# Finer first weight loads and a new order of the first and last steps in a fused attention and ELU kernel

## The chip, the cores and the metric

The kernel runs on one core of one Trainium2 chip. The metric is the device time of one execution in microseconds (us), lower is better. The profile's own span is about 1.7 us shorter than that time. PE is TensorE, PEld its weight loads, ACT is ScalarE, DVE VectorE, POOL GpSimd (which here issues loads and makes masks) and SP SyncE (which issues stores and the loads of q and k). All times inside a trace count from the start of its span.

The runs named r1 were made on one chip, r2 on a second and r3 on a third; medians are compared within one chip.

## The reference

Attention with a window of 32 on either side, then a two-layer network with ELU between its layers:

```python
scores = q @ k.T / sqrt(64); scores = where(|i - j| <= 32, scores, -1e9)
x = softmax(scores) @ v                       # 8 batches x 8 heads x 576 rows x 64
h = x.reshape(4608, 512) @ w_in               # 512 -> 2048
out = where(h > 0, h, exp(min(h, 0)) - 1) @ w_out     # 2048 -> 512
```

## The kernel before

The network part is a chain of 144 steps. A step is a tile of 256 tokens and two of the sixteen blocks of 128 hidden units. It has a first-layer product (`mm1`, 8 matmuls), an exponential (ACT), "minus one" (DVE), an ELU (DVE) and a second-layer product (`mm2`, 4 matmuls). Attention for later tokens is woven in between. PSUM has two tiles for first-layer results, taken in turn, so the `mm1` of step n must wait for the ELU of step n-2.

```python
    def mm1(kk):                      # cut
        ...                           # 8 matmuls: ps <- w_in_sb, xT
        nc.scalar.activation(e_sb, ps, AX.Exp)
        if kk == 1: nc.scalar.activation(m_sb, e_sb, AX.Copy, bias=-1.0)
        else:       nc.vector.tensor_scalar(m_sb, e_sb, -1.0, None, ALU.add)
    ...
    for kk in range(NSTEP + LAG):
        run(kk, "first")
        if 1 <= kk < NSTEP: elu(kk - 1)
        run(kk, "dve")                # attention work for DVE
        if kk < NSTEP: mm1(kk)
        run(kk, "mid")                # scores, values' products, fillers ...
        for n in {2: (), 3: (0, 1), 4: (), 5: (2, 3)}.get(kk, ...): mm2(n)
        run(kk, "end")
```

Steps 0 to 3 use the first 256 tokens, which are pairs 0 and 1 of the attention. Steps 4 to 7 use pairs 2 and 3, whose attention must be finished in between. The weights come by casting loads (float32 to bf16), a quarter of each matrix per load, all issued from POOL into one queue. "Fillers" (`idle`) are matmuls on zeros, meant to keep PE's clock up.

The softmax here doesn't subtract the row's maximum and nothing guards it: scores larger than these inputs give would overflow.

Of the kernel before, what the change touches and what calls it, by code (L numbers as in the profile page):

```python
# [21 lines left out]
def kernel(  # L22
# [9 lines left out]
    nc = tc.nc  # L32
# [6 lines left out]
    D_FF = moe_w_in.shape[1]  # L39
# [7 lines left out]
    VS = 5  # L47
# [5 lines left out]
    NFO = D_FF // 128  # L53
    FG = 2
    STEPS = NFO // FG
# [38 lines left out]
    def ps_tile(shape, dt, tag, name):  # L94
        return pools[tag].tile(shape, dt, tag=tag, name=name)
# [11 lines left out]
    w_out_sb = wpool.tile([128, NFO, D_MODEL], BF16, name="w_out_sb")  # L107
# [20 lines left out]
    def load_cast(b, which, part):  # L128
        z, nj = part
        t = cpool.tile([128, 2, nj * D], BF16, tag=f"c{which}",  # L130
                       name=f"c{which}")
        qk_c[b, which, z] = t
        src = (q, k)[which][b, :, z * NC * nj:(z + 1) * NC * nj, :].rearrange(
            "(g h) (c j) d -> c g h (j d)", h=2, j=nj)
        for h in range(2):
            nc.gpsimd.dma_start(out=t[:, h, :], in_=src[:, :, h, :])  # L136

    def load_v(b, m):
        lo = 128 * m - WIN
        p0 = max(0, -lo)  # L140
        p1 = min(128, S - lo)
        nc.gpsimd.dma_start(  # L142
            out=V_e[b % 3][p0:p1, m, :, 0:D],
            in_=v[b, :, lo + p0:lo + p1, :].rearrange("h p d -> p h d"))
# [25 lines left out]
        t = cpool.tile([1, 1], dt, name=f"gate{gates[0]}")  # L170
        eng.dma_start(out=t, in_=src)

    def load_w_in(c):
        w = D_FF // 4
        nc.gpsimd.dma_start(
            out=w_in_sb[:, :, c * w:(c + 1) * w],
            in_=moe_w_in[:, c * w:(c + 1) * w].rearrange(
                "(o p) f -> p o f", p=128))

    def load_w_out(c):  # L180
        n = NFO // 4
        nc.gpsimd.dma_start(
            out=w_out_sb[:, c * n:(c + 1) * n, :],
            in_=moe_w_out[c * n * 128:(c + 1) * n * 128, :].rearrange(
                "(o p) f -> p o f", p=128))
# [46 lines left out]
    def copy_on(eng, d_, s_):  # L232
        if eng is nc.scalar:
            nc.scalar.copy(d_, s_)  # L234
        else:
            eng.tensor_copy(d_, s_)  # L236
# [165 lines left out]

    for which in range(2):
        load_cast(0, which, HALF_B)
    load_w_in(0)
    for mi in (0, 4):
        nc.gpsimd.affine_select(
            out=masks[:, mi, :], in_=masks[:, mi, :], compare_op=ALU.is_ge,
# [4 lines left out]
        channel_multiplier=-1)  # L413
    for m in (3, 4):
        load_v(0, m)
    load_w_in(1)
    load_w_out(0)
    load_w_out(1)

    idle(10, "y1")  # L420
    front_cast(0, HALF_A, nc.vector)
# [26 lines left out]
    for which in range(2):  # L448
        load_cast(1, which, HALF_A)
    load_w_in(2)  # L450
    load_w_out(2)
    for m in range(3):
        load_v(1, m)
# [15 lines left out]
    def at(kk, slot, fn, *args):  # L469
        tasks.setdefault((kk, slot), []).append((fn, args))  # L470

    def run(kk, slot):
        for fn, args in tasks.get((kk, slot), ()):
            fn(*args)
# [9 lines left out]

    at(0, "mid", scores, 2, "s")
    at(0, "mid", scores, 3, "u")
    for i in (2, 3):
        at(0, "mid", exponential, i)
    for i in (2, 3):
        at(0, "mid", rotate_v, 0, 2, VS - 1, (i - 2,))  # L490
        at(0, "mid", mask, i)

        at(1, "mid", idle, (4, 2)[i - 2], "y1")
        at(1, "mid", pv, i)
        at(2, "dve", normalize, i)
        at(3, "mid", x_transpose, i)
        at(3, "mid", x_evac, i, nc.scalar)
    at(1, "end", idle, 1, "y1")
    at(4, "dve", swap_pools)

    for part, kq in ((HALF_A, 7), (HALF_B, 15)):
# [20 lines left out]
    for i in range(4, NPAIR):  # L522
        two = i >= FIRST_TWO
        kk, z = begin[i], i % 2 if two else 0
# [5 lines left out]
        n = kk + (3 + z if two else 2)  # L530
# [55 lines left out]
    psH, m_t, g_t, psY = {}, {}, {}, {}  # L586

    def mm1(kk):
        t, s = order[kk]
        h = kk % 2  # L590


        tags = (f"h{h}", "s") if kk == NSTEP - 1 else (f"h{h}",)
        w = FG // len(tags)
        psH[kk], m_t[kk] = [], []
        for z, tag in enumerate(tags):
            ps = ps_tile([128, w, TT], FP32, tag, "ps")
            psH[kk].append(ps)
            for j in range(w):
                fo = s * FG + z * w + j  # L600
                for do in range(NDO):
                    nc.tensor.matmul(  # L602
                        ps[:, j, :],
                        lhsT=w_in_sb[:, do, fo * 128:(fo + 1) * 128],
                        rhs=xT[t][:, :, do, :],
                        start=(do == 0), stop=(do == NDO - 1))
        for z, ps in enumerate(psH[kk]):
            e_sb = mpool.tile([128, w, TT], FP32, tag="e_sb", name="e_sb")
            nc.scalar.activation(e_sb, ps, AX.Exp)  # L609
            m_sb = mpool.tile([128, w, TT], BF16, tag="m_sb", name="m_sb")  # L610
            if kk == 1:

                nc.scalar.activation(m_sb, e_sb, AX.Copy, bias=-1.0)
            else:
                nc.vector.tensor_scalar(m_sb, e_sb, -1.0, None, ALU.add)  # L615
            m_t[kk].append(m_sb)
            if kk == NSTEP - 1:
                elu(kk, z)

    def elu(kk, z=0):  # L620
        if z == 0:
            g_t[kk] = mpool.tile([128, FG, TT], BF16, tag="g_sb", name="g_sb",
                                   bufs=5)
        ps = psH[kk][z]
        w = ps.shape[1]
        nc.vector.scalar_tensor_tensor(  # L626
            g_t[kk][:, z * w:(z + 1) * w, :], ps, 0.0, m_t[kk][z],
            ALU.max, ALU.min)

    out_t = out.rearrange("(t ts p) c -> t p ts c", p=128, ts=TT // 128)  # L630

    def mm2(kk, parts=(0, 1)):
        t, s = order[kk]
        if s == 0:
            psY[t] = [ps_tile([128, D_MODEL], FP32, g, "psY")
                      for g in (("h2", "t0") if t == 1 else ("y0", "y1"))]
        last = t == NT - 1 and s == STEPS - 1
        for ts in parts:
            for j in range(FG):
                nc.tensor.matmul(  # L640
                    psY[t][ts],
                    lhsT=g_t[kk][:, j, ts * 128:(ts + 1) * 128],
                    rhs=w_out_sb[:, s * FG + j, :],
                    start=(s == 0 and j == 0),
                    stop=(s == STEPS - 1 and j == FG - 1))
        if last and s == STEPS - 1:


            for ts in parts:
                for z in range(1 + ts):  # L650
                    c = slice(z * D_MODEL // 2 * ts,
                              D_MODEL if z == ts else D_MODEL // 2)
                    eng = (nc.vector, nc.scalar)[z]
                    y_sb = opool.tile([128, D_MODEL], FP32,
                                      tag=f"y_sb{1 - z}", name="y_sb")
                    copy_on(eng, y_sb[:, c], psY[t][ts][:, c])
                    (nc.scalar if z else nc.sync).dma_start(
                        out_t[t, :, ts, c], y_sb[:, c])
        elif s == STEPS - 1:
            for ts in range(2):  # L660
                eng = (nc.scalar, nc.vector)[ts]
                y_sb = opool.tile([128, D_MODEL], FP32, tag=f"y_sb{ts}",
                                  name="y_sb")
                copy_on(eng, y_sb, psY[t][ts])
                nc.sync.dma_start(out_t[t, :, ts, :], y_sb)

    LAG = 2
    for kk in range(NSTEP + LAG):
        run(kk, "first")
        if 1 <= kk < NSTEP:  # L670
            elu(kk - 1)
        run(kk, "dve")
        if kk < NSTEP:
            mm1(kk)
        run(kk, "mid")

        for n in {2: (), 3: (0, 1), 4: (), 5: (2, 3)}.get(
                kk, (kk - LAG,) if kk >= LAG else ()):

            if n < NSTEP - 2:  # L680
                mm2(n)
            elif n == NSTEP - 1:
                for ts in range(2):
                    for m in (n - 1, n):
                        mm2(m, (ts,))
        run(kk, "end")


# [28 lines left out]
```

## Time and profile before

| | before |
|---|---|
| median of the first three timed runs | 305.61 us |
| the execution that was profiled | 306.17 us, span 304.5 |
| PE busy | 296.0 us, 97% |
| DVE, ACT busy | 80%, 55% |

Read it so: PE has work nearly all the time, so what counts is when its unbroken stretch begins and what follows its end.

### The profile page before, as it was taken

The page shows a single profiled execution, that of the slowest core. Times are in us where ns is not written, and L with a number is a line of the kernel's source. Part 1 is how long each engine was busy: PE and PEld are TensorE (multiplying, and loading weights), DVE is VectorE, ACT ScalarE, POOL GpSimd, SP SyncE. Part 2 cuts the span into 40 slices and gives each one's busy share as a digit, 9 for nine tenths or more (in the row PEclk, how much of TensorE's full clock was granted, in tenths as well). Part 3 has the DMA queues.
Part 4 walks back from the last instruction along what each step waited for, and adds up shares of the span by engine and source line. Part 5 has one row for each costly group of instructions (what it writes and reads, how often), then busy time and mean ns, then how long its engine had stood idle before and what let it go on. Part 6 is the DMA issues. An engine that isn't in the chain of part 4 may idle for free.

```text
span 304.5 us, 7644 instructions
## 1 busy us (share of the span) xinstructions
PE 296.0 (97%) x3091; PEld 197.4 (65%) x3091; DVE 242.2 (80%) x473; ACT 168.6 (55%) x254; POOL 48.6 (16%) x68
## 2 busy tenths in 40 slices
PE   8789999999999999999999999999999999999995
PEld 3456666677676666666666666666667666666662
DVE  6867688978888887988798879887988787877664
ACT  3654556778664567546754675467535353534331
POOL 8836100910003100230013001400000000000000
PEclk9999999999999999999999999999999999999999
DMA  9999999998755997999799969996921111111011
GB/s 191 177 201 205 183 272 413 295 168 182 177 176 158 297 126 187 246 319 157 164 251 303 196 157 268 325 159 116 281 57 71 34 71 34 72 37 69 2 69 70
DMA packets 92117, 52.81 MB, mean 173 GB/s; under 512 B 76594, under 2 KB 81970, under 8 KB 92082
## 3 DMA queue, kind: packets, MB, share of 16 engines
q1 hardware_dynamic: 47330, 35.61, 43.3%
q0 software_dynamic: 42880, 10.10, 40.9%
q10 hardware_dynamic: 1872, 6.62, 5.8%
q8 instruction: 24, 0.39, 0.6%
q14 instruction: 11, 0.09, 0.1%
HBM read 36.70 MB, written 15.34 MB: 171 GB/s over the span
## 4 chain that ended last, share of the span: by engine, by line
PE 90%; DMA 3%; DVE 2%; POOL 2%; ACT 1%; issue 1%; DVEq 0%; POOLq 0%; ACTq 0%
PE ps L602 41%; PE psY L640 40%; PE psS L336 4%; PE psS L304 3%; DMA w_in_sb<-in_moe_w_in_dram 3%; PE ptx L279 1%; POOL Ve L142 1%; POOL c L136 1%; PE psXT L357 1%; DVE g_sb L626 1%; ACT pu L315 1%; DVE pm L324 0%; DVE m_sb L615 0%; PE ptx L274 0%; ACT e_sb L609 0%
## 5 line engine op out<-in xcount | busy, mean ns | idle before, releaser
L609 ACT ACTIVATE e_sb<-ps 128x512 f32<-128x512 f32 (+1 forms) x145 | 86.3, 595 | 120.6 <-PE ps L602 113.0
L602 PE MATMUL ps<-xT,w_in_sb 128*128 128x256 bf16 x1152 | 149.2, 273 | 1.4 <-DMA w_in_sb<-in_moe_w_in_dram 1.4
L640 PE MATMUL psY<-w_out_sb,g_sb 128*128 128x512 bf16 x576 | 147.6, 380 | 0.2 <-DVE g_sb L626 0.2
L602 PEld LDWEIGHTS <-w_in_sb 128*128 128x128 bf16 x1152 | 110.6, 98 | 39.7 <-DMA w_in_sb<-in_moe_w_in_dram 1.9
L626 DVE SCALAR_TENSOR_TENSOR g_sb<-ps,m_sb 128x512 bf16<-128x512 f32 (+1 forms) x145 | 99.4, 686 | 12.6
L615 DVE TENSOR_SCALAR m_sb<-e_sb 128x512 bf16<-128x512 f32 x144 | 62.5, 434 | 38.3 <-ACT e_sb L609 36.5
L640 PEld LDWEIGHTS <-g_sb 128*128 128x128 bf16 x576 | 54.5, 98 | 39.0 <-DVE g_sb L626 0.6
L142 POOL DMA_DIRECT2D Ve<-in_v_dram x40 | 35.4, 897 | 139.7 <-PE psS L336 79.9
L315 ACT ACTIVATE pu<-psS 128x1024 bf16<-128x1024 f32 x36 | 36.5, 1021 | 1.4 <-PE psS L304 1.4
L348 DVE TENSOR_TENSOR x_st<-psS,rc 128x512 bf16<-128x512 f32 x36 | 24.9, 692 | 1.2
L324 DVE TENSOR_TENSOR pm<-pu,masks 128x1024 bf16<-128x1024 bf16 x36 | 24.6, 683 | 0.6 <-ACT pu L315 0.5
L234 ACT CAST qkb<-f 128x768 bf16<-128x768 f32 (+1 forms) x29 | 25.0, 860 | 0.0
L336 PEld LDWEIGHTS <-pm 128*64 128x64 bf16 x576 | 11.2, 111 | 9.9 <-DVE pm L324 8.7
L336 PE MATMUL psS<-Ve,pm 128*64 128x65 bf16 x320 | 13.6, 197 | 0.9 <-DVE pm L324 0.9
L236 DVE COPY y_sb<-psY 128x512 f32<-128x512 f32 (+1 forms) x19 | 12.7, 671 | 1.0 <-PE psY L640 1.0
L304 PEld LDWEIGHTS <-kT 64*128 64x128 bf16 x576 | 9.5, 95 | 4.9 <-issue 4.0
L336 PE MATMUL psS<-Vo,pm 128*64 128x65 bf16 x256 | 12.0, 196 | 0.2 <-DVE Vo L153 0.2
L304 PE MATMUL psS<-qT,kT 64*128 64x64 bf16 x576 | 11.8, 191 | 0.5 <-DVE kT L236 0.5
L234 ACT COPY y_sb<-psY 128x512 f32<-128x512 f32 (+1 forms) x18 | 10.3, 571 | 3.0 <-DVE y_sb L236 3.0
L153 DVE COPY Vo<-Ve 64x1040 bf16<-64x1040 bf16 x24 | 10.3, 431 | 1.5 <-DMA Ve<-in_v_dram 0.8
L395 PE MATMUL ps_idle<-zeros 128*128 128x512 bf16 x27 | 9.5, 482 | 1.3 <-DVE zeros L194 1.3
L234 ACT COPY qT<-ptx 128x1152 bf16<-128x1152 bf16 (+2 forms) x8 | 7.5, 971 | 3.9 <-PE ptx L279 3.0
(36 smaller groups left out, 72.4 us busy)
## 6 DMA issues: line engine op xcount, KB each, us to landing
out_dram<-y_sb SPq DMA_DIRECT2D x35, 256.0 KB, 3.5
f<-in_q_dram SPq DMA_DIRECT2D x12, 576.0 KB, 5.6
f<-in_k_dram SPq DMA_DIRECT2D x12, 576.0 KB, 7.9
in_dram<-qkb ACTq DMA_DIRECT2D x10, 576.0 KB, 3.9
Ve<-in_v_dram POOLq DMA_DIRECT2D x24, 128.0 KB, 11.0
w_in_sb<-in_moe_w_in_dram POOLq DMA_DIRECT2D x4, 512.0 KB, 9.9
w_out_sb<-in_moe_w_out_dram POOLq DMA_DIRECT2D x4, 512.0 KB, 12.8
Ve<-in_v_dram POOLq DMA_DIRECT2D x16, 96.0 KB, 10.5
```

Source lines behind the costliest of these rows:

```text
L142: nc.gpsimd.dma_start(out=V_e[b % 3][p0:p1, m, :, 0:D], in_=v[b, :, lo + p0:lo + p1, :].rearrange("h p d -> p h d"))
L234: nc.scalar.copy(d_, s_)
L304: nc.tensor.matmul(psS[:, h % 2, hp * 128 + z * QB:hp * 128 + (z + 1) * QB], lhsT=kT[b % 2][base:base + 64, KPAD + hp * S + QB * qb - WIN: ...
L315: nc.scalar.activation(pu, _bap(psS, [psS.ap[0], [1, 1024]]), AX.Exp, scale=SCALE)
L324: nc.vector.tensor_mul(pm, pu, _bap(mm, [mm.ap[0], [0, H], [1, 2 * QB]]))
L336: nc.tensor.matmul(psS[QB * z:QB * (z + 1), par, hp * VD:(hp + 1) * VD], lhsT=pm[:, par * HP + hp, z * QB:(z + 1) * QB], rhs=vv[:, qb // 2 ...
L348: nc.vector.tensor_mul(x_st, _bap(psS, [psS.ap[0], [VD, HP], [512, 2], [1, D]]), _bap(rc, [rc.ap[0], [2, HP], [1, 2], [0, D]]))
L602: nc.tensor.matmul(ps[:, j, :], lhsT=w_in_sb[:, do, fo * 128:(fo + 1) * 128], rhs=xT[t][:, :, do, :], start=(do == 0), stop=(do == NDO - 1))
L609: nc.scalar.activation(e_sb, ps, AX.Exp)
L615: nc.vector.tensor_scalar(m_sb, e_sb, -1.0, None, ALU.add)
L626: nc.vector.scalar_tensor_tensor(g_t[kk][:, z * w:(z + 1) * w, :], ps, 0.0, m_t[kk][z], ALU.max, ALU.min)
L640: nc.tensor.matmul(psY[t][ts], lhsT=g_t[kk][:, j, ts * 128:(ts + 1) * 128], rhs=w_out_sb[:, s * FG + j, :], start=(s == 0 and j == 0), sto ...
```

## The change

Intent: the first product waits for a quarter of w_in although it uses an eighth of the matrix. So the first half of each matrix is loaded by eighths, which are just what a step needs. Steps 2 and 3 then go ahead of the values' products of pairs 2 and 3. ELUs 0 and 1 go ahead of pair 3's mask on DVE. Step 2's "minus one" goes to ACT. The second product of step 2 is done before step 4. At the end, one more matmul of the last step but one moves in front of the matmul that waits for the last ELU.

```diff
-    load_w_in(0)
+    for c in (0, 1):
+        load_w_in(c, 8)
 ... # mask selections, values 3 and 4
-    load_w_in(1)
-    load_w_out(0)
-    load_w_out(1)
+    for c in (2, 3):
+        load_w_in(c, 8)
+    for c in range(4):
+        load_w_out(c, 8)
 ...
+    at(0, "mid", exponential, 2)
+    at(1, "dve", rotate_v, 0, 2, VS - 1, (0,))
+    at(1, "dve", mask, 2)
+    at(1, "dve", rotate_v, 0, 2, VS - 1, (1,))
+    at(1, "mid", exponential, 3)
+    at(1, "mid", idle, 5, "y1")
+    at(2, "dve", mask, 3)
+    at(2, "mid", pv, 2)
+    at(2, "mid", normalize, 2)
+    at(3, "mid", pv, 3)
+    at(3, "mid", normalize, 3)
     for i in (2, 3):
+        at(3, "mid", lambda n: mm2(n), i - 2)
         at(3, "mid", x_transpose, i)
         at(3, "mid", x_evac, i, nc.scalar)
 ...
-            if kk == 1:
+            if kk in (1, 2):
 ...
-        for n in {2: (), 3: (0, 1), 4: (), 5: (2, 3)}.get(
+        for n in {2: (), 3: (2,), 4: (), 5: (3,)}.get(
 ...
-                for ts in range(2):
-                    for m in (n - 1, n):
-                        mm2(m, (ts,))
+                mm2(n - 1, ((0, 0), (0, 1), (1, 0)))
+                mm2(n, ((0, 0), (0, 1)))
+                mm2(n - 1, ((1, 1),))
+                mm2(n, ((1, 0), (1, 1)))
```

The old lines that put pairs 2 and 3 into the schedule are cut.

More of the change, by code (lines that the diff above doesn't have):

```diff
@@ L171, in gate, with load_w_in @@
         eng.dma_start(out=t, in_=src)
-    def load_w_in(c):
-        w = D_FF // 4
+    def load_w_in(c, of=4):
+        w = D_FF // of
         nc.gpsimd.dma_start(
@@ L178, in load_w_in, with load_w_out @@
                 "(o p) f -> p o f", p=128))
-    def load_w_out(c):
-        n = NFO // 4
+    def load_w_out(c, of=4):
+        n = NFO // of
         nc.gpsimd.dma_start(
@@ L486 @@
     at(0, "mid", scores, 3, "u")
-    for i in (2, 3):
-        at(0, "mid", exponential, i)
-    for i in (2, 3):
-        at(0, "mid", rotate_v, 0, 2, VS - 1, (i - 2,))
-        at(0, "mid", mask, i)
-        at(1, "mid", idle, (4, 2)[i - 2], "y1")
-        at(1, "mid", pv, i)
-        at(2, "dve", normalize, i)
+    at(0, "mid", exponential, 2)
[9 more added lines that the diff above has]
+    at(3, "mid", normalize, 3)
+    for i in (2, 3):
+        at(3, "mid", lambda n: mm2(n), i - 2)
         at(3, "mid", x_transpose, i)
         at(3, "mid", x_evac, i, nc.scalar)
-    at(1, "end", idle, 1, "y1")
     at(4, "dve", swap_pools)
@@ L630, with mm2 @@
     out_t = out.rearrange("(t ts p) c -> t p ts c", p=128, ts=TT // 128)
-    def mm2(kk, parts=(0, 1)):
+    def mm2(kk, parts=((0, 0), (0, 1), (1, 0), (1, 1))):
         t, s = order[kk]
@@ L637, in mm2 @@
         last = t == NT - 1 and s == STEPS - 1
-        for ts in parts:
-            for j in range(FG):
-                nc.tensor.matmul(
-                    psY[t][ts],
-                    lhsT=g_t[kk][:, j, ts * 128:(ts + 1) * 128],
-                    rhs=w_out_sb[:, s * FG + j, :],
-                    start=(s == 0 and j == 0),
-                    stop=(s == STEPS - 1 and j == FG - 1))
+        for ts, j in parts:
+            nc.tensor.matmul(
+                psY[t][ts],
+                lhsT=g_t[kk][:, j, ts * 128:(ts + 1) * 128],
+                rhs=w_out_sb[:, s * FG + j, :],
+                start=(s == 0 and j == 0),
+                stop=(s == STEPS - 1 and j == FG - 1))
         if last and s == STEPS - 1:
-            for ts in parts:
+            for ts in sorted({ts for ts, _ in parts}):
                 for z in range(1 + ts):
```

## The prediction

> **What bounds the kernel now.** I read the table of stretches first, cutting the span where the timeline shows TensorE change its work. Columns: us, then busy us and count for PE, PEld, DVE, ACT and POOL, then clock, DMA share and GB/s.
>
> ```profile
> 14.80:16.17 1.37, 0.00 (x0) 0.00 (x1) 0.29 (x1) 0.00 (x0) 0.00 (x0) 1.00 2.04 182
> 16.17:21.50 5.33, 5.11 (x88) 3.29 (x89) 3.49 (x7) 3.55 (x5) 2.61 (x4) 1.00 1.28 201
> 21.50:25.57 4.07, 4.07 (x34) 2.79 (x32) 3.79 (x9) 2.16 (x4) 0.86 (x1) 1.00 1.23 207
> 33.25:100.00 66.75, 66.53 (x760) 45.50 (x759) 53.84 (x105) 44.70 (x64) 13.11 (x15) 1.00 1.23 228
> 100.00:200.00 100.00, 100.00 (x1072) 67.47 (x1070) 85.49 (x169) 60.00 (x92) 13.64 (x16) 1.00 1.13 228
> 297.00:304.50 7.50, 3.72 (x21) 1.69 (x19) 3.37 (x8) 1.14 (x3) 0.00 (x0) 0.97 0.20 71
> ```
>
> From 21.5 to 297 us PE is busy practically all the time at full clock, so that stretch is a conveyor: it starts earlier or not. Only the start and the tail can change. At 14.80 us PE stops for 1.37 us. The waits of PE and the chain (start, us, what) name the reason:
>
> ```profile
> PE ps L602 <- DMA w_in_sb<-in_moe_w_in_dram: 1.4, 1, 1.4
> ...
> 7.72 8.41 DMA w_in_sb<-in_moe_w_in_dram
> 16.17 1.06 PE ps L602 x8
> ```
>
> So the first quarter of w_in, issued at 7.72, lands at 16.13; the activations xT are there at 14.77 (the second xT copy starts at 14.19 and takes 0.58). Then, between 16.17 and 21.50, 7 filler matmuls keep PE apparently busy: 4 + 2 + 1, on the timeline:
>
> ```profile
> 18.61 1.03 PE L395 MATMUL ps_idle<-zeros 128*128 128x512 bf16 x4
> ...
> 20.35 0.60 PE L395 MATMUL ps_idle<-zeros 128*128 128x512 bf16 x2
> ...
> 21.50 1.91 PE L602 MATMUL ps<-xT,w_in_sb 128*128 128x256 bf16 x16
> ...
> 25.57 1.91 PE L602 MATMUL ps<-xT,w_in_sb 128*128 128x256 bf16 x16
> ```
>
> Steps 0 and 1 are done by 18.8, and steps 2 and 3 begin only at 21.5. The tail, from the timeline:
>
> ```profile
> 299.62 1.25 PE L640 MATMUL psY<-w_out_sb,g_sb 128*128 128x512 bf16 x5 [0.16 <-DVE g_sb L626]
> 300.05 0.69 DVE L236 COPY y_sb<-psY 128x512 f32<-128x512 f32 x1 [0.48 <-PE psY L640]
> ...
> 300.91 0.42 DVE L236 COPY y_sb<-psY 128x256 f32<-128x256 f32 x1 [0.17 <-PE psY L640]
> 301.37 0.37 ACT L234 COPY y_sb<-psY 128x256 f32<-128x256 f32 x1 [3.00 <-DVE y_sb L236]
> ```
>
> The view that decides how far the start can move is the DMA one, taken in short windows. Two packet rates (windows of 6 to 8 and of 20 to 22 us):
>
> ```profile
> DMA packets 2188, 0.28 MB, mean 139 GB/s; under 512 B 2185, under 2 KB 2188, under 8 KB 2188
> ...
> DMA packets 418, 0.41 MB, mean 206 GB/s; under 512 B 15, under 2 KB 418, under 8 KB 418
> ```
>
> The first is mostly the values (128 B packets), the second weights (1 KB). All these casting loads share POOL's queue, which moves some 205 GB/s in the weights' stretch without a pause from 10 to 30 us. Landing times, issue plus time to landing of each transfer: second keys part 12.9, w_in quarter 0 16.13, values 3 and 4 17.6 and 18.2, w_in quarter 1 20.27, w_out quarters 0 and 1 22.82 and 25.87. That is the order of issue, as in one line: adding bytes in that order and comparing with what the queue had moved, quarter 0's last byte goes at about 14.2 and quarter 1's at 18.4, each landing some 1.9 us later.
>
> **What the Trainium skill says.** "DMA: Bandwidth & Descriptors", section "Queues, rings and completion order": descriptors of one ring are consumed in ring order; the landings above agree. Its section "Anatomy of one DMA — SWDGE (gpsimd) path" gives a fixed cost of about 2.0 us, mostly completion; my 1.9 us behind the last byte agrees. Its "Specifications" put line rate at 512 B and above. The eighths of w_in write exactly 512 B per row; no run yet shows that size. "TensorE: Matmul & The Clock Gate", section "What's actually happening": the clock drops after an idle window of about 3.4 us; the 1.37 us pause here left the clock at 1.00, and I expect no pause above 1 us.
>
> **The change, part by part.** *Loads by eighths.* One step of two hidden blocks needs 256 columns of w_in and two row blocks of w_out: precisely one eighth. Bytes and queue order are unchanged, so the landing of the last eighth of each old quarter stays, and the first of each pair comes half the quarter's transfer earlier. Cost of smaller packets: a 128 B packet takes 14.6 ns of an engine (16 engines x 2 us / 2188), a 1 KB one 77 ns; in a straight line, 512 B takes about 42. An estimate: two of them cost some 6 ns more than one of 1 KB, times 64 per engine for both quarters of w_in, 0.36 us. The w_out eighths keep 1 KB packets. Estimated landings: e0 14.7 (quarter 0's transfer takes 2.6 us; half of it off 16.13, plus a little), e1 16.3, e2 19.3 (between 18.2 and 20.27), e3 20.6, w_out 0 to 3: 21.9, 23.2, 24.7, 26.2.
>
> POOL issues more: one w_in issue is 0.79 us, so the three mask selections end near 10.1 instead of 9.33; the first mask product on DVE starts at 10.53. It fits, by 0.4 us. The build shows POOL waiting, at every issue, for the transfer issued eight before; later issues thus slip by up to 3 us (w_in quarter 2 from 18.62 to about 22), but the queue still holds some 4 us of work before it, so its landing (30.8) moves by 0.4 only, and PE needs it about 32.3.
>
> *PE's order.* The first product starts at 14.85, when xT and e0 are both there: 1.3 us gained. Then (0.98 for 8 matmuls with its start, 0.87 later, 0.28 for a pair's scores): step 0 and scores to 16.4; step 1, with e1, to 17.3; 5 fillers to 18.4; step 2 waits for e2, 19.3 to 20.2; values' product 2 (0.4) to 20.6; step 3, with e3, to 21.5; product 3 to 21.9; second product 0 (0.87) to 22.8; transpose 2 to 23.0; second product 1, with w_out 1, 23.2 to 24.1; transpose 3 to 24.3; second product 2 waits for w_out 2 and runs 24.7 to 25.6.
>
> DVE and ACT keep up: ELU 0 (mask multiply no longer ahead of it) near 17.7, mask 2 near 19.1, ELU 1 near 19.9, mask 3 20.6 and ELU 2 near 22.4, all ahead of their users. ACT gets one 0.63 us copy (step 2's minus one) from DVE, in a stage where it is half idle.
>
> PE therefore stands at 25.6, where it stood at 25.57 before, but with one second product (4 x 0.216 = 0.87) more done. Gain at the start: 25.57 + 0.87 - 25.57, **about 0.85 us**. The 1.3 us of the first wait are not a gain in themselves: half is given back in waits for later eighths. Two fillers fewer (7 to 5, 0.43) are inside this sum.
>
> *Tail.* The matmul that waits for the last ELU half stays at 299.62. After it 3 matmuls are left instead of 4, as (1,0) of the step before has moved ahead into idle time. The last ends 0.22 earlier, at 300.65. But DVE is copying the first half of the output until 300.74, so its next copy moves from 300.91 to 300.76: **0.15 us**, passed on through ACT's copy and the last store.
>
> Sum: 1.0 us. 305.6 - 1.0 = 304.6; I take 304.5, since PE could run ahead a little more if w_out 2 lands before 24.7.
>
> **The rivals.** *PE's own chain decides.* If the eighths land in good time, the same work without waits takes 9.8 us from 14.85 with the extra product: 24.65, against 25.57 + 0.87; gain 1.8, with the tail 1.95: 303.6. For it: landings of the first halves could be better than a straight line. Against it: the queue is full, and no byte is removed. *The queue decides wholly.* If the smaller transfers cost more than my line says (say 0.2 us each for eight), w_out 2 lands beyond 25.3 and the start gains under 0.3; with the tail 305.2. For it: 1816 packets in the 14 to 16 us window, many small ones, moved only 174 GB/s. Against: the boundaries between w_in 1, w_out 0 and w_out 1 show no lost time. *The gain is given back later*, because w_in quarters 2 and 3 (30.8, 38.3) don't move: 305.4. Against: before, their users start at 33.25 and 42.22, over 2 us of slack each. *A delayed mask* holds up the whole first pair: up to 0.8 us worse, 305.3.
>
> **Range and chances.** Most weight lies on a gain of 0.6 to 1.5; the full-chain rival gets a seventh, the three that return it a fifth together. So 303.6 to 305.3. 2% is 6.1 us; the whole idle time of PE is 8.5, mostly unavoidable at the ends, so faster by over 2% is nearly excluded, and nothing in the change adds 6 us.
>
> **What would show it.** Right: first w_in product near 14.9; waits of step 2 and of second product 2 on DMA, some 0.5 to 1 us each; the pair of steps after it still near 25.6; DVE's last copy 0.15 after less idle. Wrong: no wait on w_out 2 (first rival); w_out transfers landing after 25.3 (second); a PE wait on w_in near 31 or 40 us (third); a first mask product after 10.6 (fourth).

## The result, and the profile after

Five rounds: 305.32 us median (305.08 to 306.55), before 305.57 (305.34 to 305.97). The ratio is 0.9999, 95% interval 0.9978 to 1.002. A ratio is the mean time of one kernel's fast runs over that of the other's of the same rounds, so it is not quite the ratio of the medians; one run of 306.55 weighs on it. Two further sets of five rounds gave the changed kernel medians of 305.28 and 305.30, beside 305.53 and 305.58. So the medians gained about 0.25 us each time, where 1.1 had been forecast. None of the three ratios is clear of 1, since a few long runs of the changed kernel weigh on its means. All outputs are right.

The trace of after seems to contradict this, as its span is 303.7 against 304.5. Here is PE in its timeline (start us, busy us, engine, line, operation, count, and in brackets the idle time before it with what ended it). Line 609 is the first product, 396 the fillers, 358 the transposes, 646 the second product.

```profile
14.69 1.03 PE L609 MATMUL ps<-xT,w_in_sb 128*128 128x256 bf16 x8
16.23 1.05 PE L609 MATMUL ps<-xT,w_in_sb 128*128 128x256 bf16 x8
17.33 1.03 PE L396 MATMUL ps_idle<-zeros 128*128 128x512 bf16 x4
19.13 1.05 PE L609 MATMUL ps<-xT,w_in_sb 128*128 128x256 bf16 x8 [0.77 <-DMA w_in_sb<-in_moe_w_in_dram]
...
23.91 0.39 PE L358 MATMUL psXT<-ident,x_st 128*128 128x128 bf16 x4
24.31 1.02 PE L646 MATMUL psY<-w_out_sb,g_sb 128*128 128x512 bf16 x4
25.17 1.91 PE L609 MATMUL ps<-xT,w_in_sb 128*128 128x256 bf16 x16
26.92 1.03 PE L646 MATMUL psY<-w_out_sb,g_sb 128*128 128x512 bf16 x4
28.15 1.03 PE L609 MATMUL ps<-xT,w_in_sb 128*128 128x256 bf16 x8 [0.20 <-DVE g_sb L633]
```

The waits of PE in the same trace (engine, line, what it waited for, us in total, times, longest) have the same two, and the 1.4 of before is 0.8:

```profile
PE ps L609 <- DMA w_in_sb<-in_moe_w_in_dram: 0.8, 1, 0.8
...
PE ps L609 <- DVE g_sb L633: 0.2, 1, 0.2
```

Step 0 starts at 14.69 without a wait for weights. Step 2 waits for its eighth until 19.13. Second product 2 (24.31) has no bracket, since the views leave out gaps under 0.15 us and the matmuls overlap, but it too waits for weights: the last transpose is issued at 24.08 and matmuls there follow each other by 0.056, so it could have started at 24.14; its eighth of w_out (w_out 2) landed at 24.27 by the packed trace. In all six traces of the changed order that kept this place for it (after, r1_after, r3_after, r3_start, r2_halved, and r2_quarters with its quarter) second product 2 starts 0.04 us after that landing, step 4 0.90 and step 6 3.88 after it. Steps 4 and 5 run from 25.17, and step 6 starts at 28.15. In the trace of before, step 6 started at 29.04. Between 26.92 and 28.15 there are 1.23 us where the four matmuls take 0.87: 0.36 us are lost to a new wait. The chain of waits of after (start us, us, what) tells what PE waited for:

```profile
26.25 0.61 ACT e_sb L616
...
26.88 0.44 DVE m_sb L622
...
27.41 0.70 DVE g_sb L633
...
28.15 1.03 PE ps L609 x8
```

This is step 4's exponential, minus one and ELU, which frees the PSUM tile for step 6. Before, two second products (1.72 us) lay between steps 5 and 6 and covered that chain; now there is one.

From step 6 on both kernels run alike: the last first-layer product starts 267.86 to 267.88 us after step 6 in all traces of before and of the changed kernel. So one execution is the start of step 6 plus a constant, and only step 6's start and the tail need explaining. (In five traces of other variants it is 267.75 to 268.04; the table has them. Why was not looked into.)

The tail of after (SPq and ACTq are issues of stores):

```profile
298.71 0.55 PEld L646 LDWEIGHTS <-g_sb 128*128 128x128 bf16 x4 [0.43 <-DVE g_sb L633]
299.14 1.07 DVE L237 COPY y_sb<-psY 128x512 f32<-128x512 f32 x2 [0.49 <-PE psY L646]
299.86 0.81 SPq L663 DMA_DIRECT2D out_dram<-y_sb  x2
300.25 0.37 ACT L235 COPY y_sb<-psY 128x256 f32<-128x256 f32 x1 [2.78 <-DVE y_sb L237]
300.65 0.36 ACTq L663 DMA_DIRECT2D out_dram<-y_sb  x1
```

DVE's two copies now follow each other without the gap of 0.17, as forecast. The last store is issued 4.64 us after the last first-layer product starts (296.01). Its two issues in the trace of before:

```profile
300.77 0.93 SPq L657 DMA_DIRECT2D out_dram<-y_sb  x2
...
301.77 0.36 ACTq L657 DMA_DIRECT2D out_dram<-y_sb  x1
```

There it was 4.85 us (from 296.92). So 0.21 us are gained up to the last issue. But from that issue to the end of the span (taken to three places from the packed trace) it takes 3.08 us after and 2.69 before. The DMA view has the larger part of it, the time from issue to landing, before and after:

```profile
out_dram<-y_sb ACTq DMA_DIRECT2D x1, 128.0 KB, 1.8
...
out_dram<-y_sb ACTq DMA_DIRECT2D x1, 128.0 KB, 2.0
```

### The profile page after: what moved, and what is told of

It reads as the page before. It is cut to its first block, busy times and chain, and to the rows that moved or that the text cites. A ratio compares the mean times of both kernels' runs of the same rounds, so it can differ in the third digit from the quotient of the medians.

```text
span 303.7 us, 7586 instructions
## 1 busy us (share of the span) xinstructions
PE 292.5 (96%) x3035; PEld 197.3 (65%) x3089; DVE 241.6 (80%) x472; ACT 169.6 (56%) x255; POOL 51.1 (17%) x72
## 4 chain that ended last, share of the span: by engine, by line
PE 89%; POOL 3%; DMA 3%; DVE 2%; issue 1%; ACT 1%; DVEq 0%; POOLq 0%
PE ps L609 41%; PE psY L646 39%; PE psS L337 4%; PE psS L305 3%; DMA w_in_sb<-in_moe_w_in_dram 3%; POOL Ve L142 1%; PE ptx L280 1%; POOL c L136 1%; PE psXT L358 1%; DVE g_sb L633 1%; POOL w_in_sb L176 0%; PE ptx L275 0%; ACT e_sb L616 0%; ACT pu L316 0%; DVE m_sb L622 0%
## 5 line engine op out<-in xcount | busy, mean ns | idle before, releaser
L646 PE MATMUL psY<-w_out_sb,g_sb 128*128 128x512 bf16 x525 | 139.4, 379 | 2.9 <-issue 0.5
L622 DVE TENSOR_SCALAR m_sb<-e_sb 128x512 bf16<-128x512 f32 (+1 forms) x143 | 61.5, 430 | 37.5 <-ACT e_sb L616 35.6
L237 DVE COPY y_sb<-psY 128x512 f32<-128x512 f32 (+1 forms) x19 | 12.7, 671 | 0.8 <-PE psY L646 0.8
L396 PE MATMUL ps_idle<-zeros 128*128 128x512 bf16 x22 | 8.2, 494 | 1.4 <-DVE zeros L195 1.3
```

Of the source, the lines that this page charges most:

```text
L646: nc.tensor.matmul(psY[t][ts], lhsT=g_t[kk][:, j, ts * 128:(ts + 1) * 128], rhs=w_out_sb[:, s * FG + j, :], start=(s == 0 and j == 0), sto ...
```

## The experiments

Three theories were set against each other. A: the trace of before is typical, the gain of about 0.9 us at the start and 0.2 in the tail is real, and scatter hides it. B: the trace of before caught a slow execution, and a usual one already starts earlier. C: the tail's gain is given back when the stores complete.

The traces in one table. "First" is the start of step 0's product, "6 to last" runs from step 6 to the last first-layer product, "store to end" from the issue of the last store to the end of the span. The time is that of the profiled execution itself.

| trace | first | step 6 | step 6 - first | time | time - step 6 | 6 to last | store to end |
|---|---|---|---|---|---|---|---|
| before, first trace | 16.17 | 29.04 | 12.87 | 306.17 | 277.13 | 267.88 | 2.69 |
| r1_before | 15.97 | 29.29 | 13.32 | 306.42 | 277.13 | 267.87 | 2.69 |
| r2_before | 15.21 | 28.25 | 13.04 | 305.38 | 277.13 | 267.88 | 2.69 |
| r1_tail (new tail) | 15.03 | 28.05 | 13.02 | 305.24 | 277.19 | 267.88 | 2.96 |
| after (new tail) | 14.69 | 28.15 | 13.46 | 305.44 | 277.29 | 267.86 | 3.08 |
| r1_after (new tail) | 14.80 | 27.77 | 12.97 | 305.11 | 277.34 | 267.88 | 3.08 |
| r3_after (new tail) | 14.84 | 27.96 | 13.12 | 305.30 | 277.34 | 267.87 | 3.08 |
| r3_start | 14.72 | 27.96 | 13.24 | 305.20 | 277.24 | 267.86 | 2.81 |
| r1_eighths (clock low for a while) | 16.40 | 29.61 | 13.21 | 306.65 | 277.04 | 267.76 | 2.70 |
| r3_eighths | 14.73 | 27.59 | 12.86 | 304.63 | 277.04 | 267.75 | 2.68 |
| r2_quarters (new tail) | 15.45 | 28.86 | 13.41 | 306.34 | 277.48 | 268.04 | 3.09 |
| r2_earlier_xt (new tail) | 14.73 | 27.52 | 12.79 | 304.60 | 277.08 | 267.75 | 2.97 |
| r3_xt_oldtail | 14.73 | 27.53 | 12.80 | 304.56 | 277.03 | 267.75 | 2.68 |

The times, five rounds each except r2_before; the kernel before was timed in the same rounds:

| run | median | before | ratio, 95% interval |
|---|---|---|---|
| r1_before | 305.49 | 305.53 | 1.0008 (0.9992 to 1.0023) |
| r1_after | 305.28 | 305.53 | 1.001 (0.9991 to 1.0028) |
| r1_tail | 305.32 | 305.53 | 0.9999 (0.9987 to 1.0011) |
| r1_eighths | 305.24 | 305.53 | 0.999 (0.9978 to 1.0003) |
| r2_earlier_xt | 304.98 | 305.37 | 0.9988 (0.9975 to 1.0001) |
| r2_halved | 305.82 | 305.37 | 1.0019 (1.0006 to 1.0032) |
| r2_quarters | 306.46 | 305.37 | 1.0036 (1.0021 to 1.005) |
| r3_start | 305.19 | 305.58 | 0.9998 (0.9981 to 1.0016) |
| r3_xt_oldtail | 304.56 | 305.58 | 0.9973 (0.9961 to 0.9985) |
| r3_after | 305.30 | 305.58 | 0.9989 (0.9977 to 1.0002) |
| r3_eighths | 305.08 | 305.58 | 0.9986 (0.9974 to 0.9998) |

### Is the trace of before typical? r1_before and r2_before

No edit: the kernel before, profiled twice more.

> The kernel before, unchanged, against itself. Theory A (the trace of before on record is a typical fast run; the change gains about 0.9 us ahead of the conveyor and 0.2 in the tail in every run, and single runs scatter by some 0.5 us): the trace shows the step after the first four second products (the third group of products of the first layer after 25 us) starting at 29.0 again, a span of 304.5, ratio 1.000 within 0.1%. Theory B (that trace was a slow one by chance; a typical run of before is ahead of it by 0.5 us or more): the same group starts at 28.5 or earlier and the span is 303.9 or less.

> A third look at the kernel before. Theory B (the first weights' wait of 1.4 us belongs to slow executions; in most executions of before the first quarter lands near 15.0 to 15.4): if this execution takes 305.7 or less, its first product starts at 15.6 or earlier and the third group of first-layer products after 24 us (step 6) starts at 28.6 or earlier; if it takes 306 or more, they start near 16 and 29. In every case step 6 comes 12.9 to 13.3 after the first product, and the last first-layer product 267.9 after step 6. Theory A: a run of 305.5 with a first product at 16.

The first came out as theory A has it, with step 6 at 29.29, but that execution took 306.42 us, above all eleven timed runs of before in those rounds (304.87 to 305.69). (Of r1_before's own five further runs one took 306.07.) The second took 305.38, an ordinary time. Its PE timeline:

```profile
15.21 1.03 PE L602 MATMUL ps<-xT,w_in_sb 128*128 128x256 bf16 x8
...
20.71 1.91 PE L602 MATMUL ps<-xT,w_in_sb 128*128 128x256 bf16 x16
24.78 1.91 PE L602 MATMUL ps<-xT,w_in_sb 128*128 128x256 bf16 x16
...
28.25 1.04 PE L602 MATMUL ps<-xT,w_in_sb 128*128 128x256 bf16 x8
```

No bracket stands behind the first line: PE did not wait for w_in, which had landed at 15.02. It was released by the xT copy, which ended at 15.17, later than in the first trace (14.77). Step 6 came at 28.25 instead of 29.04. In all three traces the time less step 6 is the same 277.13. So theory B holds: the wait of 1.4 us that the change was to remove was there in the two slow executions and not in the usual one. The quarter landed 8.4 and 8.2 us after its issue in the slow traces, 7.5 in r2_before and 7.2 in r1_tail, whose start is that of before. In r1_tail the first product did wait for it, but for 0.20 us only (start 15.03, xT there at 14.81).

What makes it land late is settled in part. By 14 us the casting queue had moved 1.39 MB in r1_before and 1.44 MB in r1_tail (sums over windows of 1 us), which at 0.2 MB per us is worth 0.25 us; the landing differs by 1.0. The views used here do not part the queue by DMA engine, but the packed trace keeps the sixteen signals that make up one landing. Thirteen of them are in by 14.79 and 15.01 in the slow traces, by 14.48 and 14.69 in r2_before and r1_tail. Then the first trace waits for its last one until 16.12 (fifteen were in by 15.08), and r1_before for its last three from 15.74 to 15.93; the other two have all sixteen by 15.02 and 14.98. So one or three of the sixteen parts of the transfer lag. Why they do stays open.

### The changed kernel again: r1_after and r3_after

No edit.

> The changed kernel, unchanged, with five rounds. Theory A: 0.8 to 1.1 us below before (ratio 0.9965 to 0.9975). Theory B: 0.2 to 0.5 below (0.9985 to 0.9993), with its trace as before (first product near 14.7, the waiting group at 28.15).

> The changed kernel a third time, for the others of this call and for its distance to before: median 0.1 to 0.4 below before, with step 6 at 27.7 to 28.2.

The medians lie 0.25 and 0.28 below before. That is theory B's figure. The ratio of r1_after missed the expected range, because two of its six runs took 306.54 and 306.66. So the changed kernel has slow executions too. Over all sets, six of the 49 runs of kernels with loads by eighths took over 306.5, and none of the 50 with quarters and the old order did (306.42 at most). That suggests that the eighths bring such executions more often, but no run was made to show it.

### The tail alone: r1_tail

```diff
 # before, with these lines of the change alone (and mm2 taking single halves)
+                mm2(n - 1, ((0, 0), (0, 1), (1, 0)))
+                mm2(n, ((0, 0), (0, 1)))
+                mm2(n - 1, ((1, 1),))
+                mm2(n, ((1, 0), (1, 1)))
```

> Before with the last products' order alone. Both theories: 0.2 us gained between the end of the last first-layer product and the issue of the last store. If a longer completion of the last store gives it back (theory C; the time from the issue of the last store to the end was 2.4 us in the trace of before and 2.7 in that of after), the whole span gains nothing.

The last store was issued 4.64 us after the last first-layer product (300.57 - 295.93), 0.21 earlier than before's 4.85, and from there the span took 2.96 instead of 2.69. Theory C holds: the last store was in flight for 1.97 us instead of 1.76. The first of the three stores is issued 3.85 us after the last first-layer product with either tail, and the last one lands 6.6 us after that product with either tail (303.53 - 296.92 before, 302.54 - 295.93 here), so hastening the last issue alone moved nothing. Another 0.06 us is lost after the landing (0.99 us to the end instead of 0.93): SP checks the stores one after the other, and with the new tail the last landing is not the last check.

The table's two groups by tail (277.11 and 277.29 on average) must not be set against each other, since they differ in the start as well. Pairs that differ in the tail alone are r1_tail and before (277.19 and 277.13), the changed kernel and r3_start (277.29 to 277.34 and 277.24), and r2_earlier_xt and r3_xt_oldtail (277.08 and 277.03): the new tail costs 0.05 to 0.10 us in all. A further 0.11 us between the last landing and the end belongs to the changed kernel with either tail (r3_start takes 1.04 us there, where before takes 0.93). In after, r1_after, r3_after, r3_start and r2_quarters ACT's last DRAIN of the closing sequence takes 0.12 to 0.14 us, in all other traces 0.01; why is not known.

### One first store in halves: r2_halved

```diff
 # after, with the first output tile copied and stored as two halves, DVE and ACT
-                for z in range(1 + ts):
-                    c = slice(z * D_MODEL // 2 * ts,
-                              D_MODEL if z == ts else D_MODEL // 2)
+                for z in range(2):
+                    c = slice(z * D_MODEL // 2, (z + 1) * D_MODEL // 2)
```

> The changed kernel with the first output tile copied and stored in two halves as well. Theory: the end is set by 512 KB of stores that run without a pause from the first store on (1.5 us of transfer), so the first store's start decides: it is issued 0.27 us earlier and the span ends 0.25 earlier (305.05). Rival: the last store's issue decides: it stays at about 4.6 us after the last first-layer product starts, or comes later, and nothing is gained or 0.1 is lost.

The first store was issued 3.59 us after the last first-layer product's start instead of 3.85, yet the median lies 0.45 above that of before (the changed kernel itself was not in these rounds). Its store issues:

```profile
299.42 0.98 SPq L662 DMA_DIRECT2D out_dram<-y_sb  x2
...
299.83 0.36 ACTq L662 DMA_DIRECT2D out_dram<-y_sb  x1
...
300.68 0.34 ACTq L662 DMA_DIRECT2D out_dram<-y_sb  x1
```

ACT's copies wait for DVE's, so the last store leaves at 300.68, 4.85 after the last first-layer product (295.83), and the span ends 3.57 after that. My theory that the first store's start decides has fallen for these four stores; with three it fits, as r1_tail shows. The rival's figure of 0.1 lost was too small as well. That four stores ended later than three is what this one run shows, and not why.

### The start alone: r3_start

```diff
 # after, with the old tail
-                mm2(n - 1, ((0, 0), (0, 1), (1, 0)))
-                mm2(n, ((0, 0), (0, 1)))
-                mm2(n - 1, ((1, 1),))
-                mm2(n, ((1, 0), (1, 1)))
+                for ts in range(2):
+                    for m in (n - 1, n):
+                        mm2(m, ((ts, 0), (ts, 1)))
```

> The changed kernel with the old order of the last products: the start alone. In the traces so far, the time less the start of step 6 was 277.13 in three traces of before (old tail) and 277.08 to 277.48, mean 277.28, in five with the new tail. If the new tail truly gives back what it saves, this run's time less its step 6 is 277.0 to 277.2, its median 0.1 to 0.2 below the changed kernel of the same rounds. Rival (the tail's saving of 0.2 is real and the difference chance): 277.3 to 277.5 and 0.2 above the changed kernel.

The median is 305.19, 0.11 below the changed kernel of the same rounds, which is the direction of "the tail gives back". The time less step 6 is 277.24, just outside both expected ranges. Alone it would settle nothing; beside the changed kernel's own traces (277.29 to 277.34) it fits.

### The loads alone: r1_eighths and r3_eighths

```diff
 # before, with the loads of the change alone
-    load_w_in(0)
+    for c in (0, 1):
+        load_w_in(c, 8)
 ...
-    load_w_in(1)
-    load_w_out(0)
-    load_w_out(1)
+    for c in (2, 3):
+        load_w_in(c, 8)
+    for c in range(4):
+        load_w_out(c, 8)
```

> Before with the loads by eighths alone, its order kept. The first product starts at 14.8 instead of 16.17; step 1 near 16.3. The old order then keeps step 2 behind both values' products, whose second mask ends near 19.4, so step 2 near 20.3 and the first four second products wait little. If the start is bound by the second half of the loads: the products from 25 us on gain 0.5 us or less. If by the order of work: gain of 1.2 us.

> The loads by eighths alone a second time, as its first trace fell in an execution in which the clock had dropped for some us. Theory (the eighths carry the start's small gain, the new order adds next to nothing to it): in a usual execution its first product starts at 14.7 to 15.0, step 6 at 27.7 to 28.1, the time within 0.15 of the start-alone kernel. Rival (the order carries part of it): step 6 at 28.3 or later, 0.3 above the start-alone kernel.

The first trace caught an execution of 306.65 us in which the first product came 2.1 us after its weights (landed at 14.31). Its first product:

```profile
16.40 1.30 PE L604 MATMUL ps<-xT,w_in_sb 128*128 128x256 bf16 x8
```

Eight matmuls took 1.30 us there and 1.03 to 1.05 in the other traces, so PE was slower at that moment. The mean granted clock of that run was 0.992, in the other traces 0.997 to 1.0; the trace has it at 0.50 from 13.5 to 16.9 us. PE had been busy for 1.70 of the 3.41 us before that (2.31 in r3_eighths), and its longest pause there was 1.44 us. So a drop does not need the idle window of about 3.4 us that the prediction took from its page; the pause of 1.37 us in the first trace of before left the clock at 1.00. What brought it about was not tried. The other slow executions of kernels with eighths were not traced, so whether they are of this kind is open. The second trace was not disturbed, but it is the lowest of its run's five times (304.63 of 304.63 to 305.39):

```profile
14.73 1.03 PE L604 MATMUL ps<-xT,w_in_sb 128*128 128x256 bf16 x8
16.27 1.05 PE L604 MATMUL ps<-xT,w_in_sb 128*128 128x256 bf16 x8
...
20.04 1.91 PE L604 MATMUL ps<-xT,w_in_sb 128*128 128x256 bf16 x16
24.11 1.91 PE L604 MATMUL ps<-xT,w_in_sb 128*128 128x256 bf16 x16
...
27.59 1.04 PE L604 MATMUL ps<-xT,w_in_sb 128*128 128x256 bf16 x8
```

With the old order, step 6 starts at 27.59, a little before the 27.7 expected and 0.66 before r2_before; but that compares the run's fastest execution with an ordinary one. The medians are the safer measure: 305.24 and 305.08 lie 0.29 and 0.50 below before. This is at least what the whole change gained. The new order and the new tail together add nothing to it: from the medians less 277.04, step 6 of this kernel is typically at 28.0 to 28.2 (an estimate), and the new order has it at 27.77 to 28.15 in its traces.

### The order alone: r2_quarters

```diff
 # after, with the loads by quarters again
-    for c in (0, 1):
-        load_w_in(c, 8)
+    load_w_in(0)
 ... # likewise w_in 1 and w_out 0, 1
```

> The changed kernel with its loads by quarters again. If the eighths carry the gain of the start: step 2 waits for the whole second quarter of w_in, second product 0 for a whole quarter of w_out and second product 2 for the next, so step 6 starts 0.8 to 1.2 us later than in the changed kernel and the time is 306.1 to 306.5. If the order alone carries it: 305.3 to 305.6.

The time rose by 1.09 in the median beside before, in the upper part of the first expectation. The new order calls for each weight earlier, and quarters bring it later; second product 2 started 0.04 after its quarter of w_out landed (24.97), while second product 0 did not wait for its own, against the expectation:

```profile
15.45 1.05 PE L607 MATMUL ps<-xT,w_in_sb 128*128 128x256 bf16 x8 [0.64 <-DMA w_in_sb<-in_moe_w_in_dram]
...
19.95 1.05 PE L607 MATMUL ps<-xT,w_in_sb 128*128 128x256 bf16 x8 [0.82 <-DMA w_in_sb<-in_moe_w_in_dram]
```

### Taking the new wait away: r2_earlier_xt and r3_xt_oldtail

```diff
 # after; pair 3's normalization no longer behind step 3's "minus one" on DVE
-            if kk in (1, 2):
+            if kk in (1, 2, 3):
 ...
+    at(3, "mid", lambda n: mm2(n), 0)
     for i in (2, 3):
-        at(3, "mid", lambda n: mm2(n), i - 2)
         at(3, "mid", x_transpose, i)
         at(3, "mid", x_evac, i, nc.scalar)
+    at(3, "mid", lambda n: mm2(n), 1)
 ...
-        for n in {2: (), 3: (2,), 4: (), 5: (3,)}.get(
+        for n in {2: (), 3: (), 4: (), 5: (2, 3)}.get(
```

> The changed kernel with pair 3's normalization no longer behind step 3's minus one on DVE (that goes to ACT), its transpose ahead of second product 1, and second product 2 back behind step 5. Theory: the changed order gives back 0.35 us because step 6 waits for ELU 4. If so, that wait goes, step 6 starts 12.5 to 12.7 after the first product instead of 13.0 to 13.4, and the time falls 0.4 below the changed kernel (304.9). Rival: the second-layer weights' landings bind, so step 6 stays where it was (within 0.15) and a wait on w_out appears.

> The best start found (pair 3's transpose earlier) with the old tail. Step 6 starts near 27.4 to 27.6; time 0.3 to 0.7 below before of the same rounds, 304.7 to 305.0, and the lowest of this call. If the new tail is the better one, it lies 0.1 to 0.2 above the earlier run of the same start (304.98).

The wait for ELU 4 is gone, and with it the one for w_out 2, as second product 2 is back behind step 5; these runs do not part the two. Two second products fill the time again, and step 6 follows without a pause (r3_xt_oldtail):

```profile
25.81 1.89 PE L647 MATMUL psY<-w_out_sb,g_sb 128*128 128x512 bf16 x8
27.53 1.04 PE L610 MATMUL ps<-xT,w_in_sb 128*128 128x256 bf16 x8
```

Step 6 starts 12.8 us after the first product, not the 12.5 to 12.7 expected, but earlier than in any of the changed kernel's traces (12.97 to 13.46). With the old tail the median is 304.56, 1.02 below before, more than the 0.3 to 0.7 expected, and 0.74 below the changed kernel of the same rounds. It is the best version found, and the interval of its ratio, 0.9961 to 0.9985, is clear of 1. Beside r2_earlier_xt (304.98, another chip, 0.39 below its before) it is the lower one with the old tail; but the two traces differ by only 0.05 from step 6 to the end, so most of that distance is not the tail's and stays unexplained.

## Why the prediction was wrong

**"At 14.80 us PE stops for 1.37 us" and "1.3 us gained" at the first product: the step that failed.** The figure is right for the trace it came from. But that execution took 306.17 us, and I took the gain off the 305.6 of the timed runs. In r2_before and r1_tail, of ordinary length, the first product starts at 15.21 and 15.03 and waits for weights by 0 and 0.20. Measured from there the changed kernel's first product comes 0.2 to 0.5 earlier (14.69 to 14.84), and step 6 at 27.77 to 28.15 against 28.25 and 28.05. From the medians, less the constants 277.13 and 277.32, step 6 is typically at 28.44 before and 28.00 after (305.57 and 305.32): an estimate of 0.44 gained at the start, where I had 0.85.

**PE's place in the changed kernel: right in its waits, lucky at step 6.** Step 0 at 14.85 was predicted and 14.69 came; step 2 at 19.3, and 19.13 came, after a wait on its eighth; the pair of steps at 25.6, and 25.17 came. For step 6 the forecast gain means 28.2, and 28.15 came; but this agreement is luck, as two errors of about 0.4 cancel. The landings came earlier than estimated (eighth 0 at 13.86 instead of 14.7, w_out 2 at 24.27 instead of 24.7), and a wait that I did not have took 0.36 back. Against the trace of before, 29.04, the start gained 0.89 us, about what I had worked out: the error is in the start it was measured from.

**The wait on w_out 2: right, but smaller.** I had 0.4 us for it, and 0.5 to 1 us in its sign; it took 0.18, and the landing paces steps 4 to 6 in six traces. Beside it came a wait that no step of mine had, for ELU 4 ahead of step 6 (0.36 us). I counted the advanced second product as a plain gain of 0.87 and did not ask what it had covered.

**The tail's 0.15 us: wrong in its last link.** The copies moved as worked out (the gap of 0.17 went, and the last store's issue came 0.21 earlier). "Passed on through ... the last store" did not hold: the last store was in flight for 0.21 us longer, and the tail cost 0.05 to 0.10 in sum.

**Three sums of the working are off.** The list of PE's work from 14.85 to 25.6 holds waits of 0.9, 0.2 and 0.4, so the same work without waits takes about 9.25 us and not the 9.8 of the first rival. Half of 2.6 us off 16.13, plus a little, is 14.8 or later and not 14.7. And "1.9 us behind the last byte" takes the queue to move bytes strictly in order; the first of quarter 0's sixteen signals came at 14.03, before the 14.2 worked out, and the last at 16.12, so the 1.9 is mostly the spread of the parts, and it does not confirm the fixed cost that the prediction cites.

**The rivals.** "The queue decides wholly" gave 305.2, near the result, but for another reason: it needed w_out 2 to land beyond 25.3, and it landed at 24.27 and paced PE from there. "PE's own chain decides" is out by its own sign, since second product 2 did wait. "Given back later" and "a delayed mask" are out: before and the changed kernel both took 267.9 us from step 6 to the last first-layer product, and the first mask product of after starts at 10.23. The rival that was missing is that the profiled execution might not stand for the timed ones. The time of the profiled execution was there to be compared with the median, and it was the warning.

Sum: 0.44 gained at the start and 0.19 lost after step 6 (the tail's 0.05 to 0.10 and the 0.11 after the last landing), 0.25 in all. The 0.44 is worked out from the medians, so the sum must agree; the traces alone bear it out only within 0.1 lost to 0.5 gained.

## What to carry to other kernels

Compare the time of the profiled execution with the median of the timed runs before any wait in its trace is counted as a gain; when they differ by as much as the gain hoped for, take a second trace. When work is moved out of a place, ask what it covered there: the second product moved ahead laid bare a chain of product, exponential, minus one and ELU of 2.98 us (step 4's start to step 6's). And a gain up to the last store's issue is a gain only when the end of the span moves with it. To price one part of a change, compare runs that differ in that part alone.

## What the Trainium skill lacked or had wrong

- "DMA: Bandwidth & Descriptors", section "Anatomy of one DMA — SWDGE (gpsimd) path", gives the fixed cost of a load as about constant. Here the same first load of 512 KB, in the same place of its queue, landed 7.2, 7.5, 8.2 and 8.4 us after its issue in four executions, with little difference in what the queue had moved. No page gives a size for how far the last of a load's sixteen signals can lag: here 1.04 us behind the fifteenth in one execution, 0.05 in another. What the prediction took from its "Specifications" agrees: while the eighths of w_in with their 512 B rows passed (11 to 14 us), the queue moved 0.19 to 0.20 MB per us, close to the 0.20 to 0.21 of the 1 KB rows.
- "Perfetto Trace Analysis", section "Identifying Performance Opportunities", says how to find what blocks an engine, but not to check that the traced execution is a usual one. Here it was 0.6 us above the median, more than the whole gain.
- No page that I read says that hastening the last store alone can gain nothing: with three stores issued over 1.0 us the last was in flight for 1.76 to 1.77 us, over 0.8 us for 1.97 to 1.99, so that it landed 6.6 us after the last first-layer product either way; with four stores it took 2.21.
